# Top-32 attention into routed experts: row scans folded to half width, mask and product moved to GpSimd, row sums to ScalarE

## The chip, the core and the metric

The kernel runs on one core of one Trainium2 chip. The metric is device time in microseconds: the median of five runs, and beside it one execution taken with the profiler, whose trace the readings come from. Engines are named as the profile names them: PE (TensorE), PEld (its weight loads), DVE (VectorE), ACT (ScalarE), POOL (GpSimd), SP (SyncE, which issues most DMAs).

## The reference

Inputs are float32: `q`, `k`, `v` of 8 batches x 8 heads x 576 rows x 64, a gate of 512 x 8, and for 8 experts `w1` (512 x 1024) and `w2` (1024 x 512).

```python
scores = scale * np.matmul(q, k.transpose(0, 1, 3, 2))
kth = np.partition(scores, -32, axis=-1)[..., -32:-31]
scores = np.where(scores >= kth, scores, -1e9)
attn = np.exp(scores - scores.max(-1, keepdims=True))
attn = attn / (attn.sum(-1, keepdims=True) + 1e-09)
x = matmul(attn, v), heads side by side          # 4608 x 512
expert = argmax(x @ w_gate); gate = its softmax probability
out = gate * (relu(x @ w1[expert]) @ w2[expert])
```

So in each of 36,864 score rows of 576 the 32nd largest value is a threshold; what lies below it gets no weight.

## The kernel before

**Attention.** Two heads share the 128 partitions; a unit is one pair of heads of one batch, 32 units in all. A unit's 1152 query rows make nine tiles of 128 rows: four groups of two (the same chunk of both heads), and one single tile that holds the last 64 rows of both. For each group `scores` multiplies q and k into PSUM (L182) and ScalarE copies the 128 x 576 result to SBUF as `s` (L188). `weights` finds the threshold on DVE: four rounds of MAX8 (L200, the eight largest of a row) with three match-replaces between them (L205, which overwrite those eight). After the first round GpSimd makes the bias from the row maximum (L202), and ScalarE computes the exponential `ex` (L203). DVE then compares, multiplies and sums in one instruction, `w = (s >= threshold) * ex` with its row sum in `z` (L212).

`transposed` turns `w` on PE (four transposes at L223, the tail at L224) and ScalarE copies the results to `wT` and `wTt` (L228 to L232). After the ninth tile `outputs` multiplies with v in two halves (`po`, L253), copies to `oT` (L254), transposes back to `px` (L261) and DVE scales by the reciprocal row sums into `x` (L262, the tail at L269).

**Routing.** After every second batch `route` transposes `x` (L283), computes gate logits (L287), copies them (L291), finds each token's expert and its place, and writes token numbers to lists in HBM by nine indirect DMAs from GpSimd's queue (L326). `x` goes to HBM from SP's queue (L339, L342).

**Experts.** 25 slots of 256 tokens each: SP reads a list piece and the expert's weights, GpSimd gathers rows (L434), PE multiplies twice (L452, L459), GpSimd scatters the result (L464). Two slots are loaded ahead.

**Order.** The code asks for the scores of the next group ahead of the weights of this one, and for transposes of the last tile after the weights of this one. A scheduler then sets the order on each engine, and each engine works its queue in order. Pools bound what may run ahead: four buffers of `s`, three of `w`, two of `ex`, two score tiles in PSUM.

Of the kernel before, what the change touches and what calls it, by code (L numbers as in the profile page):

```python
# [1 line left out]

# [12 lines left out]
TOP_K = 32  # L15
NEG = -3.0e38
EPS = 1e-9


def _ins(ap: bass.AP, axis: int, n: int) -> bass.AP:  # L20
    dims = [list(d) for d in ap.ap]
    dims.insert(axis, [0, n])
    return bass.AP(tensor=ap.tensor, offset=ap.offset, ap=dims)

# [6 lines left out]
def kernel(  # L31
# [9 lines left out]
):  # L41

# [70 lines left out]
    tok_id = []  # L113
    for p in range(NP):
        t = const.tile([P, NT], I32, name=f"tok_id{p}")
        b0 = 2 * p * S
        nc.gpsimd.iota(t[:, 0:NC], pattern=[[P, NC]], base=b0, channel_multiplier=1)
        nc.gpsimd.iota(t[:, NC:2 * NC], pattern=[[P, NC]], base=b0 + S, channel_multiplier=1)
        nc.gpsimd.iota(t[0:ST, 2 * NC:NT], pattern=[[1, 1]], base=b0 + SM, channel_multiplier=1)
        nc.gpsimd.iota(t[ST:P, 2 * NC:NT], pattern=[[1, 1]], base=b0 + S + SM, channel_multiplier=1)  # L120
        tok_id.append(t)

# [10 lines left out]
    cnt = None  # L133
    firstp = ctx.enter_context(tc.tile_pool(name="firstp", bufs=1))
    first_w = None

    with (
        tc.tile_pool(name="pad", bufs=1) as padp,
        tc.tile_pool(name="load", bufs=2) as load,
        tc.tile_pool(name="att", bufs=2) as att,  # L140
        tc.tile_pool(name="wtp", bufs=2) as wtp,
        tc.tile_pool(name="xp", bufs=2) as xp,
        tc.tile_pool(name="small", bufs=3) as small,
        tc.tile_pool(name="ps_s", bufs=2, space=bass.MemoryType.PSUM) as ps_s,
        tc.tile_pool(name="ps_w", bufs=2, space=bass.MemoryType.PSUM) as ps_w,
        tc.tile_pool(name="ps_1", bufs=1, space=bass.MemoryType.PSUM) as ps_1,
    ):
        qk, vs_of, xt, units = {}, {}, {}, {}

        def load_qk(b, u):  # L150
            qb = load.tile([P, 2, S], F32, name="qb")
            nc.sync.dma_start(qb, qt[b, u * P:(u + 2) * P, :].rearrange("(u p) s -> p u s", p=P))
            kb = load.tile([P, 2, S], F32, name="kb")
            nc.sync.dma_start(kb, kt[b, u * P:(u + 2) * P, :].rearrange("(u p) s -> p u s", p=P))
            for n in range(2):
                qk[b, u + n] = (qb[:, n, :], kb[:, n, :])

        def load_v(b):
            vb = load.tile([P, KC, HD], F32, name="vb")
            nc.sync.dma_start(vb[:, 0:NC, :], vt[b, 0:SM, :].rearrange("(c p) d -> p c d", p=P))  # L160
            nc.sync.dma_start(vb[0:ST, NC, :], vt[b, SM:S, :])
            vs_of[b] = vb

        def parts(i):

            if i < 2 * NC:
                h, c = divmod(i, NC)
                return [(h, slice(0, P), slice(c * P, (c + 1) * P))]
            return [(h, slice(h * ST, (h + 1) * ST), slice(SM, S)) for h in range(2)]

        def scores(b, u, tiles):
            qu, ku = qk[b, u]
            todo = []
            got = []
            for i in tiles:
                ps = ps_s.tile([P, 2, SM], F32, name="sc")
                todo += [(ps, h, rows, cols) for h, rows, cols in parts(i)]
                got.append(ps)
            for j in range(2):
                for ps, h, rows, cols in todo:  # L180
                    d = slice(h * D, (h + 1) * D)
                    nc.tensor.matmul(  # L182
                        ps[rows, j, 0:HF], qu[d, cols], ku[d, j * HF:(j + 1) * HF], start=True, stop=True
                    )
            out_s = []
            for ps in got:
                s = att.tile([P, 2, HF], F32, name="s", bufs=4)
                nc.scalar.copy(s, ps[:, :, 0:HF])  # L188
                out_s.append(s)
            return out_s  # L190

        def weights(b, u, i, s3):
            s = s3[:, :, :].rearrange("p j k -> p (j k)")
            tops = small.tile([P, TOP_K // 8, 8], F32, name="tops")
            scr = att.tile([P, S], F32, name="scr")
            nbias = small.tile([P, 1], F32, name="nbias")
            ex = att.tile([P, S], F32, name="ex")
            src = s
            for r in range(TOP_K // 8):
                nc.vector.max(out=tops[:, r, :], in_=src)  # L200
                if r == 0:
                    nc.gpsimd.tensor_scalar(nbias, tops[:, 0, 0:1], -scale, None, ALU.mult)  # L202
                    nc.scalar.activation(ex, s, AF.Exp, scale=scale, bias=nbias)  # L203
                if r < TOP_K // 8 - 1:
                    nc.vector.match_replace(  # L205
                        out=scr, in_to_replace=tops[:, r, :], in_values=src, imm_value=NEG
                    )
                    src = scr
            w = att.tile([P, S], F32, name="w", bufs=3)
            z = units[b, u][2]  # L210
            c = 2 * NC if i == 2 * NC else 2 * (i % NC) + i // NC
            nc.vector.scalar_tensor_tensor(  # L212
                out=w, in0=s, scalar=tops[:, TOP_K // 8 - 1, 7:8], in1=ex,
                op0=ALU.is_ge, op1=ALU.mult, accum_out=z[:, c:c + 1],
            )
            return w

        def transposed(b, u, i, w):
            wT, wTt, _ = units[b, u]
            pm = ps_w.tile([P, NC, P], F32, name="wTm")  # L220
            pt = ps_1.tile([P, SM], F32, name="wTl")
            for c in range(NC):
                nc.tensor.transpose(pm[:, c, :], w[:, c * P:(c + 1) * P], ident)  # L223
            nc.tensor.transpose(pt[0:ST, 0:P], w[:, SM:S], ident)  # L224
            if i < 2 * NC:
                h, c = divmod(i, NC)
                q = slice(c * P, (c + 1) * P)
                nc.scalar.copy(wT[:, :, h, q], pm)  # L228
                nc.scalar.copy(wTt[:, h, q], pt[0:ST, 0:P])
            else:  # L230
                nc.scalar.copy(wT[:, :, :, SM:S], pm[:, :, :].rearrange("p c (h q) -> p c h q", h=2))
                nc.scalar.copy(wTt[:, :, SM:S], pt[0:ST, 0:P].rearrange("p (h q) -> p h q", h=2))  # L232

        def outputs(b, u):
            vb = vs_of[b]
            wT, wTt, z = units[b, u]
            rz = small.tile([P, NT + 1], F32, name="rz", bufs=2)
            nc.vector.tensor_scalar_add(rz[:, 0:NT], z, EPS)
            nc.vector.reciprocal(rz[:, 0:NT], rz[:, 0:NT])
            nc.vector.tensor_copy(rz[0:ST, NT:NT + 1], rz[ST:P, 2 * NC:NT])  # L240
            oT = att.tile([P, S], F32, name="oT")
            for j in range(2):
                q = slice(j * HF, (j + 1) * HF)
                po = ps_1.tile([P, SM], F32, name="po")
                for c in range(KC):
                    for h in range(2):
                        rows = slice(h * D, (h + 1) * D)
                        vs = slice(u * P + h * D, u * P + (h + 1) * D)
                        if c < NC:
                            lhsT, rhs = vb[:, c, vs], wT[:, c, h, q]  # L250
                        else:
                            lhsT, rhs = vb[0:ST, c, vs], wTt[:, h, q]
                        nc.tensor.matmul(po[rows, 0:HF], lhsT, rhs, start=(c == 0), stop=(c == KC - 1))  # L253
                nc.scalar.copy(oT[:, q], po[:, 0:HF])  # L254
            p, half = divmod(b, 2)
            if u == 0 and half == 0:
                xt[p] = xp.tile([P, NT, XW], F32, name="x")
            x = xt[p]
            px = ps_1.tile([P, SM], F32, name="px", tag="po")
            for t in range(NC):  # L260
                nc.tensor.transpose(px[:, t * P:(t + 1) * P], oT[:, t * P:(t + 1) * P], ident)  # L261
            nc.vector.tensor_tensor(  # L262
                x[:, half * NC:(half + 1) * NC, u * P:(u + 1) * P].rearrange("p t (h d) -> p t h d", h=2),
                px[:, :].rearrange("p (t h d) -> p t h d", t=NC, h=2),
                _inner(rz[:, 0:2 * NC].rearrange("p (t h) -> p t h", h=2), D), op=ALU.mult,
            )
            pl = ps_1.tile([P, SM], F32, name="pl", tag="po")
# [247 lines left out]
```

## Time and profile before

| what | value |
|---|---|
| median of five runs | 2674.95 us (2673.63 to 2678.48) |
| profiled execution | 2674.07 us, its span 2672.4 us |
| mean granted TensorE clock | 0.715 |
| DVE busy | 1736.5 us (65%) |
| PE busy, PEld busy | 2039.0 us (76%), 1206.3 us (45%) |
| ACT busy | 717.4 us (27%) |
| POOL busy | 200.7 us (8%) |

A line of a group gives the source line, engine, operation, output and inputs with shapes, the count, then busy time in us and mean ns of one, then the idle time of the engine just before them and what ended it. A timeline line gives the start, the duration, and in brackets the idle time before it and the releaser. A stretch gives its borders and length, then PE, PEld, DVE, ACT and POOL busy with counts, the granted clock, the DMA share and GB/s.

### The profile page before, as it was taken

Reading aid. Unit: us, or ns where it says so; the run is one execution under the profiler, and the core shown is the slowest. Engines: PE = TensorE matmul, PEld = TensorE weight load, DVE = VectorE, ACT = ScalarE, POOL = GpSimd, SP = SyncE. Lnnn points to the kernel's source line nnn. Section 1 sums busy time; section 2 is a strip of 40 time slices with the busy share of each in tenths; the row PEclk is TensorE's granted clock in tenths of the full one; section 3 lists DMA queues with packets and bytes.
Section 4 is the critical chain, followed back from the end, with each engine's and each line's share of the span. In section 5 each row is a group of like instructions: output and inputs, shape, how many; then the busy total and the mean of one; then the engine's idle time right before and its main releaser. Section 6 shows DMA issues by size and latency. Waiting matters only on the chain. (4 is left out here: it accounts for less than half of the span.)

```text
span 2672.4 us, 22208 instructions
## 1 busy us (share of the span) xinstructions
PE 2039.0 (76%) x7208; PEld 1206.3 (45%) x7208; DVE 1736.5 (65%) x3864; ACT 717.4 (27%) x1457; POOL 200.7 (8%) x453
## 2 busy tenths in 40 slices
PE   5767767666767776677686667676199999999998
PEld 3334334333333543333353333334166666666665
DVE  8999998699999869999986999995100010010000
ACT  3333333233333323333332333332011011001100
POOL 0000000100000010000001000000111111111110
PEclk7665566566666656665665666665599999999999
DMA  3000001100000110000011000000364444545440
GB/s 136 18 18 18 18 1 36 36 18 18 18 18 0 36 36 18 18 18 18 0 36 36 18 18 0 1 0 0 116 226 161 179 174 179 181 159 198 158 155 2
DMA packets 71172, 166.84 MB, mean 62 GB/s; under 512 B 9612, under 2 KB 9740, under 8 KB 71058
## 3 DMA queue, kind: packets, MB, share of 16 engines
q1 hardware_dynamic: 61906, 142.83, 15.8%
q0 software_dynamic: 9152, 22.60, 2.2%
q8 instruction: 58, 0.95, 0.1%
q14 instruction: 56, 0.46, 0.1%
HBM read 146.34 MB, written 22.73 MB: 63 GB/s over the span
## 5 line engine op out<-in xcount | busy, mean ns | idle before, releaser
L223 PE MATMUL wTm<-ident,w 128*128 128x128 f32 x1152 | 282.3, 392 | 493.2 <-DVE w L212 476.5
L200 DVE MAX8 tops<-scr 128x8 f32<-128x576 f32 x864 | 620.1, 744 | 0.5
L182 PE MATMUL sc<-kb,qb 64*128 64x288 f32 (+1 forms) x1280 | 577.1, 656 | 30.2 <-ACT s L188 22.6
L223 PEld LDWEIGHTS wTm<-ident,w 128*128 128x128 f32 x1152 | 187.8, 199 | 670.9 <-issue 504.9
L205 DVE MATCH_REPLACE8 scr<-tops,scr 128x576 f32<-128x576 f32 x576 | 424.9, 738 | 0.0
L182 PEld LDWEIGHTS sc<-kb,qb 64*128 64x128 f32 (+1 forms) x1280 | 279.7, 269 | 202.2 <-issue 108.1
L452 PE MATMUL ph<-xTs,w 128*128 128x256 f32 x1600 | 353.9, 382 | 14.1 <-DVE xTs L447 13.5
L188 ACT COPY s<-sc 128x576 f32<-128x576 f32 x288 | 184.1, 640 | 646.7 <-DVE w L212 638.0
L459 PE MATMUL py<-w,hT 128*128 128x512 f32 x800 | 347.4, 592 | 0.0
L452 PEld LDWEIGHTS ph<-xTs,w 128*128 128x128 f32 x1600 | 303.5, 191 | 60.4 <-DVE xTs L447 19.0
L463 DVE TENSOR_SCALAR y<-py,xg 128x512 f32<-128x512 f32 x50 | 37.5, 750 | 440.8 <-PE py L459 440.8
L253 PE MATMUL po<-wT,vb 128*64 128x288 f32 x1024 | 275.5, 638 | 1.4 <-ACT wT L228 0.9
L455 ACT ACTIVATE hT<-ph 128x256 f32<-128x256 f32 x200 | 76.6, 383 | 701.7 <-PE ph L452 701.7
L203 ACT ACTIVATE ex<-s,nbias 128x576 f32<-128x576 f32 x288 | 223.8, 777 | 92.8 <-POOL nbias L202 92.7
L459 PEld LDWEIGHTS py<-w,hT 128*128 128x128 f32 x800 | 152.0, 190 | 180.7 <-issue 179.4
L212 DVE SCALAR_TENSOR_TENSOR w<-s,tops,ex 128x576 f32<-128x576 f32 x288 | 230.0, 800 | 0.1
L200 DVE MAX8 tops<-s 128x8 f32<-128x576 f32 x288 | 213.7, 743 | 8.5 <-ACT s L188 8.4
L205 DVE MATCH_REPLACE8 scr<-tops,s 128x576 f32<-128x576 f32 x288 | 212.5, 738 | 0.0
L228 ACT COPY wT<-wTm 128x512 f32<-128x512 f32 x256 | 149.9, 586 | 169.5 <-PE wTm L223 166.1
L202 POOL TENSOR_SCALAR nbias<-tops 128x1 f32<-128x1 f32 x288 | 60.5, 210 | 1665.9 <-DVE tops L200 1365.5
L253 PEld LDWEIGHTS po<-wT,vb 128*64 128x64 f32 x1024 | 108.5, 213 | 163.1 <-issue 156.9
L431 DVE TENSOR_SCALAR src<-idx 128x2 int32<-128x2 int32 x25 | 4.2, 169 | 262.4 <-DMA idx<-lists 262.4
(89 smaller groups left out, 983.4 us busy)
## 6 DMA issues: line engine op xcount, KB each, us to landing
w<-in_moe_w_dram SPq DMA_DIRECT2D x50, 2048.0 KB, 11.2
qb<-in_qt_dram SPq DMA_DIRECT2D x16, 576.0 KB, 3.9
kb<-in_kt_dram SPq DMA_DIRECT2D x16, 576.0 KB, 4.9
x_rows<-x SPq DMA_DIRECT2D x8, 1026.0 KB, 10.3
vb<-in_vt_dram SPq DMA_DIRECT2D x8, 1024.0 KB, 5.8
x_rows<-x SPq DMA_DIRECT2D x8, 128.2 KB, 10.4
vb<-in_vt_dram SPq DMA_DIRECT2D x8, 128.0 KB, 5.7
xg<-x_rows,src POOLq DMA_INDIRECT x50, 7.8
```

What stands on the lines that cost most here:

```text
L182: nc.tensor.matmul(ps[rows, j, 0:HF], qu[d, cols], ku[d, j * HF:(j + 1) * HF], start=True, stop=True)
L188: nc.scalar.copy(s, ps[:, :, 0:HF])
L200: nc.vector.max(out=tops[:, r, :], in_=src)
L203: nc.scalar.activation(ex, s, AF.Exp, scale=scale, bias=nbias)
L205: nc.vector.match_replace(out=scr, in_to_replace=tops[:, r, :], in_values=src, imm_value=NEG)
L212: nc.vector.scalar_tensor_tensor(out=w, in0=s, scalar=tops[:, TOP_K // 8 - 1, 7:8], in1=ex, op0=ALU.is_ge, op1=ALU.mult, accum_out=z[:, c: ...
L223: nc.tensor.transpose(pm[:, c, :], w[:, c * P:(c + 1) * P], ident)
L228: nc.scalar.copy(wT[:, :, h, q], pm)
L253: nc.tensor.matmul(po[rows, 0:HF], lhsT, rhs, start=(c == 0), stop=(c == KC - 1))
L452: nc.tensor.matmul(ph, w1[:, 0, dt, f * P:(f + 1) * P], xT[:, dt, :], start=(dt == 0), stop=(dt == DT - 1))
L455: nc.scalar.activation(hT[:, f, :], ph, AF.Relu)
L459: nc.tensor.matmul(py, hT[:, f, c * P:(c + 1) * P], w2[:, 0, f, :], start=(f == 0), stop=(f == FT - 1))
```

## The change

Each score row is folded: DVE writes the maximum and the minimum of `s[i]` and `s[i + 288]` to `hl`. The four rounds of MAX8 and three match-replaces run over the 288 larger members, and one more MAX8 over the smaller members. The 32nd largest of all is then the largest of nine minima: the (32 - j)th of the larger with the jth of the smaller, j from 0 to 8. This is exact while at most eight of the smaller members belong to the top 32.

The difference of the eighth smaller member and the threshold is kept in `over`, and its maximum in `doubt`. After attention this becomes a flag. After the experts each engine loads the flag and branches: where it is raised, a second copy of the kernel (full-width scans, in loops) computes everything again.

The comparison with the threshold and the product with `ex` are now two instructions on GpSimd, and the row sum is an activation on ScalarE. `weights` and the transposes work on a whole group, not on one tile; `ex` has four buffers instead of two, `scr` three instead of two, `x` one instead of two. The thresholds' scratch `tops` is four tiles used in turn. Gate, routing and expert code move into functions without other change.

```diff
+    def scores(b, u, tiles):
...
             s = k.att.tile([P, 2, HF], F32, name="s", bufs=4)
             nc.scalar.copy(s, ps[:, :, 0:HF])
+            if not k.exact:
+                hl = k.att.tile([P, 2, HF], F32, name="hl", bufs=4)
+                nc.vector.tensor_tensor(hl[:, 0, :], s[:, 0, :], s[:, 1, :], op=ALU.max)
+                nc.vector.tensor_tensor(hl[:, 1, :], s[:, 0, :], s[:, 1, :], op=ALU.min)
...
+    def weights(b, u, tiles, ss):
...
+            src = [hl[:, 0, :] for _, hl in ss]
...
+        for r in range(R):
+            for m in range(n):
+                nc.vector.max(out=tops[:, m, r * 8:(r + 1) * 8], in_=src[m])
+            if r == 0:
+                nc.gpsimd.tensor_scalar(nbias[:, 0:n], tops[:, 0:n, 0], -scale, None, ALU.mult)
+                for m in range(n):
+                    nc.scalar.activation(ex[m], s[m], AF.Exp, scale=scale, bias=nbias[:, m:m + 1])
+                if not k.exact:
+                    for m in range(n):
+                        nc.vector.max(out=tops[:, m, TOP_K + 1:TOP_K + 9], in_=ss[m][1][:, 1, :])
+            if r < R - 1:
+                for m in range(n):
+                    nc.vector.match_replace(
...
+            both = k.small.tile([P, 2, 9], F32, name="both")
+            nc.vector.tensor_tensor(
+                both[:, 0:n, :], _back(tops[:, 0:n, TOP_K - 9:TOP_K]), tops[:, 0:n, TOP_K:TOP_K + 9], op=ALU.min
+            )
+            nc.vector.tensor_reduce(thr[:, 0:n], both[:, 0:n, :], axis=AX.X, op=ALU.max)
+            nc.gpsimd.tensor_tensor(over[:, c:c + n], tops[:, 0:n, TOP_K + 8], thr[:, 0:n], op=ALU.subtract)
...
-            nc.vector.scalar_tensor_tensor(
-                out=w, in0=s, scalar=tops[:, TOP_K // 8 - 1, 7:8], in1=ex,
-                op0=ALU.is_ge, op1=ALU.mult, accum_out=z[:, c:c + 1],
-            )
+            w = k.att.tile([P, S], F32, name="w", bufs=3)
+            nc.gpsimd.tensor_scalar(w, s[m], thr[:, m:m + 1], None, ALU.is_ge)
+            nc.gpsimd.tensor_tensor(w, w, ex[m], op=ALU.mult)
+            nc.scalar.activation(ex[m], w, AF.Copy, accum_out=z[:, c + m:c + m + 1])
...
+        nc.vector.tensor_tensor(doubt, doubt, over, op=ALU.max)
...
+    again = nc.values_load(any_i[0:1, 0:1], min_val=0, max_val=P)
+    with tc.If(again > 0):
...
```

The order that the scheduler gives the changed kernel, in the steady part of a unit: DVE runs the first MAX8 of the next pair around the threshold of this one, then its fifth MAX8s and first match-replaces, then the folds of the pair after next. GpSimd runs for each pair: bias of the next pair, `over`, two comparisons, two products. ScalarE runs: one exponential, two score copies, two row sums, the second exponential, then the copies of transposes. PE runs the transposes of a pair, then scores of a later group; in two of the four pairs three score matmuls stand between the second tile's transposes and its tail transpose.

## The prediction

> **What bounds the kernel now.** I read the totals and slices first, then the stretches of time, then groups of instructions by shape, then the timeline of one pair and of one unit's end.
>
> ```profile
> PE 2039.0 (76%) x7208; PEld 1206.3 (45%) x7208; DVE 1736.5 (65%) x3864; ACT 717.4 (27%) x1457; POOL 200.7 (8%) x453
> DVE  8999998699999869999986999995100010010000
> PEclk7665566566666656665665666665599999999999
> ```
>
> Two stages show. The DVE row is nearly full for 28 of 40 slices and empty after, the clock row low, then full. Stretches of time give the borders (columns: stretch, its length, busy us with instruction counts):
>
> ```profile
> 0.00:1838.00 1838.00, 1288.23 (x4466) 703.12 (x4466) 1654.88 (x3690) 634.16 (x1244) 92.78 (x344) 0.61 0.07 22
> 1936.00:2672.00 736.00, 716.86 (x2587) 476.62 (x2585) 69.51 (x121) 76.60 (x200) 95.36 (x96) 1.00 0.45 162
> ```
>
> Attention takes about 1838 us, DVE busy 1655 of them, PE 1288 at a granted clock of 0.61. Last route, list reading and experts (1838 to 2672) keep their instructions, and I let them stand. What DVE does per row tile:
>
> ```profile
> L200 DVE MAX8 tops<-scr 128x8 f32<-128x576 f32 x864 | 620.1, 744 | 0.5
> L205 DVE MATCH_REPLACE8 scr<-tops,scr 128x576 f32<-128x576 f32 x576 | 424.9, 738 | 0.0
> L212 DVE SCALAR_TENSOR_TENSOR w<-s,tops,ex 128x576 f32<-128x576 f32 x288 | 230.0, 800 | 0.1
> L401 DVE TENSOR_TENSOR past<-slots,end 1x175 f32<-1x175 f32 x1 | 0.3, 322 | 0.0
> ```
>
> Instructions overlap by about 0.07 us: in the timeline one MAX8 starts 0.67 after another, a match-replace with its value load takes 0.72, the product 0.73. A tile is 4 x 0.67 + 3 x 0.72 + 0.73 = 5.57 us, a pair 11.14; the timeline has 721.28 to 732.40 = 11.12 between like products. Nine tiles are 50.1. Starts of the scaling at L262 (698.97, 753.57) lie 54.6 apart; of the other 4.5, 3.1 to 3.2 is one wait, the rest small work:
>
> ```profile
> 697.82 0.40 ACT L254 COPY oT<-po 128x288 f32<-128x288 f32 x1 [5.42 <-PE po L253]
> 698.97 0.69 DVE L262 TENSOR_TENSOR x<-px,rz 128x512 f32<-128x512 f32 x1 [3.20 <-PE px L261]
> ```
>
> So a unit is 54.6 us, 32 make 1747; the three routes inside stretch the spacing to 84.5, 82.1 and 84.5.
>
> **DVE after.** Removed: L212 and half the width of every scan. Halving 576 elements saves 0.30 us of each (175 elements take 0.32 us and 72 take 0.22, L316, in the two-input rows, so 1.0 ns an element): MAX8 0.37, match-replace 0.42 with its load. Added: two folds of 288, 0.32 + 113 x 0.001 = 0.43 each, 0.36 start to start, and a fifth MAX8. A tile is 2 x 0.36 + 5 x 0.37 + 3 x 0.42 = 3.83; each group adds a minimum and a maximum over 18 elements, 0.25 together by the 9-element rows (0.16 to 0.19). A pair is 7.9, the single tile 4.1, small work 1.5 with the doubt maximum: 37.2 a unit without waits.
>
> **GpSimd after.** Before, it makes one bias per tile (L202, 0.21 us for one element). No row shows a wide comparison or product there. Nearest: the 128-element select at L95 takes 0.288, the 288-element iota at L348 0.373 against 0.134 for 4, so 0.6 to 0.85 ns an element. The comparison is 0.21 + 575 x that = 0.56 to 0.70; I take 0.7, as it reads and compares like the select but by a per-row value. The product reads two operands: twice the slope, 0.9 to 1.2; I take 1.2, and 2.0 as the upper end since no two-input row bounds it. By the Trainium skill (GPSIMD Engine Reference, Elementwise — side-by-side cycle accounting), a two-input add of 2048 takes 4497 ns there; scaled, an estimate of 1.27 us, which would add 0.14 to a pair; no row here shows it. With bias and flag (0.2 each, the bias mostly early) a pair is about 4.1 us from the threshold to its second product, 19 us per unit: no bound by volume. Its place counts: it is now between DVE's threshold and PE's transposes.
>
> **ScalarE after.** The row sum is a 576-wide activation like L203 (0.777), plus a read of the accumulator (0.08 on DVE): 0.85 per tile. Per tile 0.64 + 0.78 + 0.85 + 0.59 + 0.26 = 3.1, 28 per unit: below DVE. But it waits in order for the second product, and behind it in its queue stand an exponential, the copies of transposes, and the next score copies.
>
> **The shared port.** Folds read two SBUF inputs. What that does to GpSimd shows where a scatter starts under L212, also two inputs:
>
> ```profile
> 501.04 0.80 DVE L212 SCALAR_TENSOR_TENSOR w<-s,tops,ex 128x576 f32<-128x576 f32 x1
> 501.15 1.57 POOL L326 DMA_INDIRECT lists<-tok_id,posi  x1 [4.46 <-DMA lists<-tok_id,posi]
> 520.43 0.97 POOL L326 DMA_INDIRECT lists<-tok_id,posi  x1 [2.33 <-DMA lists<-tok_id,posi]
> ```
>
> The first takes 0.6 more, and 501.04 + 0.80 - 501.15 = 0.69 of L212 was left. Five more that start under it take 1.07 to 1.23; nearly all others take 0.97 to 1.03. GpSimd stands still for the rest of L212. Under MAX8 a bias at 537.65 takes its usual 0.21. The reverse, DVE waiting for GpSimd, doesn't show: L212 at 968.45, in the middle of a scatter, starts on time and takes 0.80; but a scatter isn't elementwise work. So a fold's wait for a running GpSimd instruction is bounded by 0 and one product, 1.2. In the changed order the folds of the pair after next stand 1.6 us behind a threshold (two MAX8, two match-replaces), and their score buffers come free by the two comparisons (1.0 and 1.7), just when the products begin. I take one wait and 0.4 for a late score copy, 1.6 per pair: 9.5.
>
> In half the pairs a loop is longer: second product, transposes 1.09, three score matmuls 3.4 (2.29 for two), the tail transpose 0.42, its copy 0.26, exponential 0.78, score copy 0.64, hand-overs 0.3: 6.9 us. It must fit into a period and 1.6. With the product at 4.1 it asks 9.4, at 5.6 (one wait) 10.9; by the fast rows (1.23, 0.66, 0.27) 2.2 less, 7.2 to 8.7. I take 9.9 for those pairs, 9.7 over all.
>
> **Unit's end.** Before, 9.3 us run from the last product (689.7) to L262, 6.1 covered by DVE's next work. After, GpSimd adds 2.2 and a score matmul 0.5 to 1.1: 12 to 12.6; DVE's cover is 7.35 (ten MAX8, five match-replaces, two folds, small ones) plus 1.5 of port waits: 3.5 left.
>
> **Sum.** A unit: 4 x 9.7 + 5.2 (single, with one short wait) + 1.5 + 3.5 = 49.0 against 54.6; 32 x 5.6 = 179 off. Routes: DVE has 9.4 instead of 12 us of cover before the logits, and their nine scatters now queue ahead of comparisons and products, each waiting for the one before to land (1.9 to 4.5); bounds 0 and 20, I take 8 each, 24. The end gains a register load and a branch per engine, no row for it: 0 to 8, I take 4, since the second path is skipped. In the inputs of the reference I counted, of 36,864 rows, how many smaller pair members reach the threshold: at most 6, and 8 raise the flag. The profiled execution is 2674.07 (span 2672.4 and 1.7 around it), 0.9 below the median of the five runs, so nothing is shifted: 2674 - 179 + 24 + 4 = 2523, given as 2525.
>
> **Rivals.** (1) Full gain: folds don't wait, and denser PE work earns a higher clock. Unit 37.2 + 3 = 40.2, 32 x 14.4 = 461 off, 12 on: about 2225, up to 2400 with half the waits. For it: the L212 that started on time; PE's idle stretches of 3 to 5 us in attention would shrink, and the expert stage, where PE is busy 717 of 736 us, is granted 1.00. Against: the folds come exactly when products run. (2) Slower: DVE and GpSimd alternate, fold, product, fold, so a pair waits twice, and the second product slips to 7. Pairs are then 11.1, those with the loop 12.3, the single 6, unit's end 5: unit 59.3, 32 x 4.7 = 150 on, with 28 gives 2852; about 2800 if some pairs escape. It decides from a pair mean of 10.7 on ((53.7 - 5.5 - 1.5 - 4) / 4, with 54.6 less 28/32). A product of 2.0 instead of 1.2 leads there too. For it: GpSimd's full stop under L212. Against: neighbouring DVE instructions overlap, so the second fold may keep the port. By the Trainium skill (SBUF — State Buffer, Who interferes with whom), a DVE instruction with two SBUF inputs and a GpSimd one that reads SBUF exclude each other, whichever starts first holding the port throughout; that speaks for this rival. The scatters agree in one direction (1.57 against 0.97); the other is unseen here. (3) The flag is raised and the second path runs: at least another 2600 us; the count speaks against it.
>
> **Chances.** Forecast 0.45 (2430 to 2640), full gain 0.17, slower 0.34, second path 0.01, break-even 0.03. About 0.2%, 5 us, is what a measurement here can tell. Faster 0.62, same 0.03, slower 0.35 (with the second path). The range 2320 to 2790 leaves out half of the full gain and about 0.1 of the slow side; the forecast alone spans 2430 to 2640.
>
> **What would show it.** Right: pairs 9.3 to 10.2 apart on DVE, folds with idle before them put to GpSimd or ScalarE, MAX8 near 444 ns, GpSimd about 0.7 and 1.2, L262's wait 3 to 4. Wrong: pairs near 8 (full gain); products of 2 us, or pairs over 10.7 with the long wait at score copies (slower); instructions of the second path in the trace.

## Result

The changed kernel takes 2682.28 us (median of 31 runs, 2664.19 to 2691.65) against 2676.37 us of the kernel before (55 runs); the ratio is 1.0023, with a 95% interval of 1.0016 to 1.003. The forecast was 2525 us; the kernel came out slower by 0.2% instead of faster by 6%, inside the range and on its other side.

The profiled execution took 2680.86 us, its span 2679.0. The totals and slices of the page after:

```profile
PE 2063.3 (77%) x7210; PEld 1179.0 (44%) x7210; DVE 1410.0 (53%) x4511; ACT 910.7 (34%) x2033; POOL 1109.8 (41%) x1062
...
DVE  7777777478777747777775777774100010010000
...
PEclk9656666556566656565665565666599999999999
```

VectorE's work did go: 1410 us busy instead of 1737. GpSimd's went from 201 to 1110. But the DVE row, which stood at 8 and 9 through attention, stands at 7 for as many slices as before. The two stretches of the prediction, in its columns:

```profile
0.00:1838.00 1838.00, 1311.40 (x4461) 675.48 (x4461) 1328.21 (x4335) 824.29 (x1811) 997.60 (x950) 0.62 0.07 22
1936.00:2672.00 736.00, 719.57 (x2597) 478.66 (x2596) 71.56 (x123) 76.60 (x200) 95.15 (x96) 1.00 0.45 164
```

In the same 1838 us VectorE is busy 1328 us instead of 1655, and what it stopped doing became idle time. The clock (0.62) and the expert stretch are as before. The last scaling of `x` (L329, which was L262) starts at 1849.2 against 1846.2, and what follows takes 829.8 us against 826.2; together these are the 6.6 us of the span. The groups of instructions by shape:

```profile
L277 POOL TENSOR_SCALAR w<-s,thr 128x576 f32<-128x576 f32 x288 | 493.6, 1723 | 65.0 <-PE wTl L289 65.0
...
L278 POOL TENSOR_TENSOR w<-w,ex 128x576 f32<-128x576 f32 x288 | 410.0, 1441 | 3.4
L245 DVE MAX8 tops<-scr 128x8 f32<-128x288 f32 x864 | 353.9, 444 | 0.1
...
L223 DVE TENSOR_TENSOR hl<-s 128x288 f32<-128x288 f32 x288 | 199.6, 693 | 351.9 <-ACT s L219 351.9
...
L224 DVE TENSOR_TENSOR hl<-s 128x288 f32<-128x288 f32 x288 | 181.9, 632 | 0.5
```

The scans are what was forecast. The comparison (L277) takes 1.72 us, more than the product (1.44), and the folds (L223, L224) average 0.69 and 0.63 instead of the 0.43 that was reckoned. The first fold has 352 us of idle time before it. Of the waits (engine, tile and line, what it waited for, us in total, times, longest) three lines matter:

```profile
DVE hl L223 <- ACT s L219: 351.9, 219, 10.3
...
ACT s L219 <- POOL w L277: 171.5, 157, 3.7
...
DVE x L329 <- PE px L328: 107.1, 31, 5.7
```

352 us are 11.0 us per unit, slightly more than the 327 us by which VectorE's busy time fell in attention. The second line gives the next link: ScalarE's score copies wait for the comparisons, the last readers of the score buffers. A pair in the timeline shows how it comes about (start, duration; in brackets the idle time before and its releaser):

```profile
713.29 0.14 DVE L271 TENSOR_REDUCE thr<-both 128x2 f32<-128x18 f32 x1
...
713.81 3.43 POOL L277 TENSOR_SCALAR w<-s,thr 128x576 f32<-128x576 f32 x2
...
715.57 0.64 ACT L219 COPY s<-sc 128x576 f32<-128x576 f32 x1 [1.08 <-POOL w L277]
716.24 0.46 DVE L223 TENSOR_TENSOR hl<-s 128x288 f32<-128x288 f32 x1 [1.23 <-ACT s L219]
...
717.20 2.98 POOL L278 TENSOR_TENSOR w<-w,ex 128x576 f32<-128x576 f32 x2
717.27 0.64 ACT L219 COPY s<-sc 128x576 f32<-128x576 f32 x1 [1.06 <-POOL w L277]
717.94 0.98 DVE L223 TENSOR_TENSOR hl<-s 128x288 f32<-128x288 f32 x1 [0.87 <-ACT s L219]
...
718.84 1.66 DVE L224 TENSOR_TENSOR hl<-s 128x288 f32<-128x288 f32 x1
...
725.10 0.15 DVE L271 TENSOR_REDUCE thr<-both 128x2 f32<-128x18 f32 x1
```

The threshold is computed at 713.29. VectorE goes on with the next pair's first scans until 715.01; then the folds of the pair after next stand in its order. Their score copies need the two buffers that the comparisons still read, until about 715.5 and 717.2. Each copy starts as a comparison ends, and each first fold starts as its copy ends: 1.23 and 0.87 us idle. By now the products run, and the last two folds take 0.98 and 1.66 us. From threshold to threshold it is 11.81 us. The working closes: 7.9 without waits, 2.10 idle, 1.76 in which those two folds hold up what follows (0.90 and 1.58 from start to start instead of 0.36 each), 11.76 together.

### The profile page after: what moved, and what is told of

It is laid out like the page before. It is cut to its first block, busy times and chain, and to the rows that moved or that the text cites. A ratio compares the mean times of both kernels' runs of the same rounds, so it can differ in the third digit from the quotient of the medians.

```text
span 2679.0 us, 24033 instructions
## 1 busy us (share of the span) xinstructions
PE 2063.3 (77%) x7210; PEld 1179.0 (44%) x7210; DVE 1410.0 (53%) x4511; ACT 910.7 (34%) x2033; POOL 1109.8 (41%) x1062
## 5 line engine op out<-in xcount | busy, mean ns | idle before, releaser
L213 PE MATMUL sc<-kb,qb 64*128 64x288 f32 (+1 forms) x1280 | 568.6, 649 | 255.4 <-ACT s L219 248.0
L277 POOL TENSOR_SCALAR w<-s,thr 128x576 f32<-128x576 f32 x288 | 493.6, 1723 | 65.0 <-PE wTl L289 65.0
L213 PEld LDWEIGHTS sc<-kb,qb 64*128 64x128 f32 (+1 forms) x1280 | 253.1, 259 | 462.6 <-ACT s L219 297.0
L278 POOL TENSOR_TENSOR w<-w,ex 128x576 f32<-128x576 f32 x288 | 410.0, 1441 | 3.4
L223 DVE TENSOR_TENSOR hl<-s 128x288 f32<-128x288 f32 x288 | 199.6, 693 | 351.9 <-ACT s L219 351.9
L245 DVE MAX8 tops<-scr 128x8 f32<-128x288 f32 x864 | 353.9, 444 | 0.1
L499 POOL DMA_INDIRECT out_dram<-y,idx x50 | 50.5, 1011 | 620.0 <-DVE y L498 620.0
L279 ACT ACTIVATE ex<-w 128x576 f32<-128x576 f32 x288 | 197.3, 686 | 208.8 <-POOL w L278 208.8
L255 DVE MATCH_REPLACE8 scr<-tops,scr 128x288 f32<-128x288 f32 x576 | 250.0, 438 | 0.0
L247 POOL TENSOR_SCALAR nbias<-tops 128x2 f32<-128x2 f32 (+1 forms) x160 | 46.9, 293 | 408.0 <-DVE thr L271 366.2
L224 DVE TENSOR_TENSOR hl<-s 128x288 f32<-128x288 f32 x288 | 181.9, 632 | 0.5
## 6 DMA issues: line engine op xcount, KB each, us to landing
w<-in_moe_w_dram SPq DMA_DIRECT2D x50, 2048.0 KB, 10.7
```

Source lines behind the costliest of these rows:

```text
L213: nc.tensor.matmul(ps[rows, j, 0:HF], qu[d, cols], ku[d, j * HF:(j + 1) * HF], start=True, stop=True)
L223: nc.vector.tensor_tensor(hl[:, 0, :], s[:, 0, :], s[:, 1, :], op=ALU.max)
L245: nc.vector.max(out=tops[:, m, r * 8:(r + 1) * 8], in_=src[m])
L255: nc.vector.match_replace(out=scr[m], in_to_replace=tops[:, m, r * 8:(r + 1) * 8], in_values=src[m], imm_value=NEG,)
L277: nc.gpsimd.tensor_scalar(w, s[m], thr[:, m:m + 1], None, ALU.is_ge)
L278: nc.gpsimd.tensor_tensor(w, w, ex[m], op=ALU.mult)
```

## Experiments

Theory A: GpSimd's comparison is slow by itself, holds the score buffers and delays the products. Theory B: GpSimd's work on SBUF stretches VectorE's folds through the shared port. Theory C: folded scans bring nothing here. Theory D was formed after the first runs: four score buffers leave the copies no lead, so that whatever is late on their way stops VectorE.

**Folds alone.** Mask, product and row sum are one VectorE instruction again.

```diff
-            nc.gpsimd.tensor_scalar(w, s[m], thr[:, m:m + 1], None, ALU.is_ge)
-            nc.gpsimd.tensor_tensor(w, w, ex[m], op=ALU.mult)
-            nc.scalar.activation(ex[m], w, AF.Copy, accum_out=z[:, c + m:c + m + 1])
+            nc.vector.scalar_tensor_tensor(
+                out=w, in0=s[m], scalar=thr[:, m:m + 1], in1=ex[m],
+                op0=ALU.is_ge, op1=ALU.mult, accum_out=z[:, c + m:c + m + 1],
+            )
```

> The changed kernel with the comparison, product and row sum back in one DVE instruction; folded scans, flag and second path stay. Theory A (GpSimd's long comparison holds the loop up) and theory B (folds and GpSimd exclude each other at the shared port) both expect DVE to set the pace: a tile 3.83 + 0.73 = 4.56 us, a unit 9 x 4.56 + 1.3 + 1.5 + 3 = 47, so 32 x 7.6 = 243 off the kernel before, 2440. If the folded scans themselves brought nothing (theory C: waits inside the scans), it would stay over 2600.

Measured: 2418.01 us, ratio 0.9011 (0.8989 to 0.9032). C falls: the folded scans are worth a tenth of the time, and moving the mask away gives it back. Both folds average 0.45 us, and VectorE's wait for score copies is 88 us in all.

**GpSimd's operations alone.** The kernel before, with comparisons, products and the like over 64, 288 and 576 elements ahead of attention, one after another.

```diff
+        for name, n in (("m64", 64), ("m288", HF), ("m576", S)):
+            tb = padp.tile([P, S], F32, name=name)
+            nc.gpsimd.tensor_scalar(tb[:, 0:n], ta[:, 0:n], ones[:, 0:1], None, ALU.is_ge)
...
+            nc.gpsimd.tensor_tensor(tb[:, 0:n], ta[:, 0:n], ta[:, 0:n], op=ALU.mult)
```

> The kernel before, with GpSimd instructions added ahead of attention, where DVE is idle: comparison and product by a per-row value and by a constant, a maximum, a subtract-and-multiply and two-input product and subtraction, each over 64, 288 and 576 elements. Theory A (the comparison is slow by itself): the comparison by a per-row value over 576 takes about 1.7 us here too, the two-input product 1.4. Theory B (the shared port stretches it): the comparison takes about 0.7 and the product 1.2, as forecast.

The groups there (L348 is the comparison by a per-row value, L353 the product):

```profile
L348 POOL TENSOR_SCALAR m<-ta,ones 128x576 f32<-128x576 f32 x1 | 1.7, 1733 | 0.0
...
L353 POOL TENSOR_TENSOR m<-ta 128x576 f32<-128x576 f32 x1 | 1.1, 1140 | 0.0
...
L348 POOL TENSOR_SCALAR m<-ta,ones 128x64 f32<-128x64 f32 x1 | 0.5, 467 | 0.1
```

This kernel takes 2693.47 us in all (one run). The comparison takes 1.73 us alone as well. VectorE is idle beside it, so its price is its own, not the port's: (1733 - 467) / 512 = 2.5 ns an element. The product, 1.14 us, is nearer to B's 1.2 than to A's 1.4.

**A short comparison.** It covers 64 of 576 columns, and the product squares the exponential: this kernel leaves out the mask.

```diff
-            nc.gpsimd.tensor_scalar(w, s[m], thr[:, m:m + 1], None, ALU.is_ge)
-            nc.gpsimd.tensor_tensor(w, w, ex[m], op=ALU.mult)
+            nc.gpsimd.tensor_scalar(w[:, 0:64], s[m][:, 0:64], thr[:, m:m + 1], None, ALU.is_ge)
+            nc.gpsimd.tensor_tensor(w, ex[m], ex[m], op=ALU.mult)
```

> The changed kernel, its comparison over only 64 of 576 columns, its product of the exponential with itself over all 576: the mask is left out, the instruction count and the order of waits stay. Theory A: score buffers come free at 0.8 us after a threshold instead of 3.8 and the second product at 3.7 instead of 6.6; the forecast's sum then holds, 2480 to 2560. Theory B: products still exclude folds, more than 2620.

Measured: 2636.92 us, ratio 0.9838 (0.9813 to 0.9862): A missed. The total misleads, though. Unit spacings, without the route units and the three behind them, fell from 54.3 to 48.3 on average, and attention ended 87.0 us earlier although those six took 479 us instead of 416. Then the time after attention was 870.5 us instead of 829.8. Without the mask the routing differs; that the longer lists and experts come from that is likely, and was not separated. The comparison's length is worth some 6 us of the 54 of a unit, less than the 11 that VectorE waits. VectorE still waits 293.5 us for score copies here, and its folds, 0.71 and 0.73 us, are stretched more than before.

**Folds from PSUM.** One half of each fold is read where the score matmul left it.

```diff
-                nc.vector.tensor_tensor(hl[:, 0, :], s[:, 0, :], s[:, 1, :], op=ALU.max)
-                nc.vector.tensor_tensor(hl[:, 1, :], s[:, 0, :], s[:, 1, :], op=ALU.min)
+                nc.vector.tensor_tensor(hl[:, 0, :], ps[:, 0, 0:HF], s[:, 1, :], op=ALU.max)
+                nc.vector.tensor_tensor(hl[:, 1, :], ps[:, 0, 0:HF], s[:, 1, :], op=ALU.min)
```

> The changed kernel, the folds reading one half of a score row from PSUM and one from SBUF, so that they have one SBUF input; everything else stays. Theory A: only the folds' own waits go, 576 folds at 0.45 are 259 of their 381 us, so at most 4 us a unit, 120 in all, and likely less as the score copies still come late: 2600 to 2680. Theory B: below 2560.

Measured: 2600.81 us, ratio 0.9698 (0.9682 to 0.9714). In its timeline a fold inside two products now takes its usual time:

```profile
730.61 2.79 POOL L278 TENSOR_TENSOR w<-w,ex 128x576 f32<-128x576 f32 x2
...
732.33 0.45 DVE L223 TENSOR_TENSOR hl<-sc,s 128x288 f32<-128x288 f32 x1
```

So the stretches need both of a fold's inputs in SBUF, as B has it. They were 199.6 + 181.9 - 576 x 0.445 = 125 us; without them the kernel gains 82. But its folds still wait 413 us for score copies, and the time is not below the 2560 that B asked for: B is real, and the smaller part.

**The comparison on VectorE.** It takes 0.51 us there.

```diff
-            nc.gpsimd.tensor_scalar(w, s[m], thr[:, m:m + 1], None, ALU.is_ge)
+            nc.vector.tensor_scalar(w, s[m], thr[:, m:m + 1], None, ALU.is_ge)
```

> The changed kernel with the comparison alone moved to VectorE (one instruction for 576 scores); the product stays on GpSimd, the row sum on ScalarE. VectorE gains 288 comparisons; a fold of half the width takes 0.45, so I estimate 0.4 to 0.8 us each, 115 to 230 us in all, or 3.6 to 7.2 us per unit. Theory A (the price of the comparison on GpSimd, 1.72 us also when it runs alone, is what cost the gain): the wait for score copies nearly goes, units of 46 to 50 us, 2420 to 2540 us. Theory B (any GpSimd work on the score rows stretches VectorE's two-input work, and the product alone is enough): folds keep means over 600 ns and the time is over 2580 us.

Measured: 2656.32 us, ratio 0.989 (0.9873 to 0.9908). A in its strong form falls: the slow comparison is gone, and plain units still take 54.0 us. The wait for score copies is 258 us, in 65 long ones:

```profile
L224 DVE TENSOR_TENSOR hl<-s 128x288 f32<-128x288 f32 x288 | 201.1, 698 | 0.4
...
L223 DVE TENSOR_TENSOR hl<-s 128x288 f32<-128x288 f32 x288 | 154.6, 537 | 258.5 <-ACT s L219 258.5
```

B's numbers came out: the folds average 0.62 us over both lines, and the time is over 2580. But the stretches, 201.1 + 154.6 - 256 = 100 us, are less than half of that wait. One of the long waits in the timeline:

```profile
726.81 0.40 ACT L321 COPY oT<-po 128x288 f32<-128x288 f32 x1 [7.38 <-PE po L320]
...
727.78 0.63 ACT L219 COPY s<-sc 128x576 f32<-128x576 f32 x1
...
728.45 0.46 DVE L223 TENSOR_TENSOR hl<-s 128x288 f32<-128x288 f32 x1 [7.11 <-ACT s L219]
```

Here the score copy stands behind the copy of an output row on ScalarE, which waits for the output matmuls. The waiting line is the same, but what stands ahead of the copy is another.

**Eight score buffers.**

```diff
-            s = k.att.tile([P, 2, HF], F32, name="s", bufs=4)
+            s = k.att.tile([P, 2, HF], F32, name="s", bufs=8)
```

> The changed kernel with eight buffers for `s` instead of four; nothing else. In the changed kernel VectorE waits 351.9 us in all for score copies, and in a plain unit the copies of a later pair begin when a comparison (1.72 us each) has let go of a score buffer, while the folds of that pair stand ahead of scans that could run. Theory A (the long comparison holds the score buffers): the 171.5 us in which ScalarE's score copies wait for comparisons go to under 30 us and the wait of the folds falls by at least 130 us, so 2500 to 2580 us. Rival (the loop of product, transposes, score matmuls and copies binds at the same place; the buffer is only the last of several that end there): the copies then wait for another releaser and the time stays at 2640 to 2700 us.

Measured: 2379.56 us, ratio 0.8862 (0.8847 to 0.8877): better than both theories allowed, and better than both kernels. Its groups:

```profile
L219 ACT COPY s<-sc 128x576 f32<-128x576 f32 x288 | 182.7, 637 | 232.4 <-POOL w L277 218.5 <-PE sc L213 12.9 <-DVE hl L224 0.8
...
L224 DVE TENSOR_TENSOR hl<-s 128x288 f32<-128x288 f32 x288 | 161.9, 562 | 0.0
...
L223 DVE TENSOR_TENSOR hl<-s 128x288 f32<-128x288 f32 x288 | 148.4, 515 | 9.5 <-ACT s L219 9.2
```

VectorE's wait for score copies is 9 us instead of 352. The comparison is still 1.74 us, and score copies wait for it longer than before (218 us against 171): in the first line the wait stays, but it costs nothing, since the copies now run ahead of the folds. The expectation looked for the gain in ScalarE's wait, which did not fall; VectorE's did. A unit is 44.4 us: 37.2 of work, 1.7 of stretched folds (148.4 + 161.9 - 256, over 32), and 2.7, 1.8 and 1.1 for the waits at L329, L305 and L336 (84.9, 56.6 and 35.3 us in all). The steps from threshold to threshold in a unit, from the second pair on (the fourth step starts at the single tile, and the last holds the unit's end), are 7.8, 7.3, 7.8, 8.3 and 13.4 where the changed kernel has 11.8, 10.0, 9.8, 7.5 and 13.9.

**The mask's move alone.** The first pass at full width, with the mask on GpSimd.

```diff
-        open_pools(st, 2, False)
+        open_pools(st, 2, True)
```

> The changed kernel with its first pass at full width: no folds, no second list, MAX8 and match-replace over 576, while the comparison and the product stay on GpSimd and the row sum on ScalarE (the second, flagged pass is the same code as before). It shows the move of the mask by itself. VectorE loses 0.90 us per tile against the kernel before (the mask instruction and its accumulator read), 8.1 us per unit, and has no two-input instruction left in a pair. If the mask's path through GpSimd binds a unit wherever the scans end (theory A in its strong form), units stay at 53 to 55 us and the time is 2640 to 2720 us. If only folds caught between comparisons and products lose time (theory B), pairs are 9.5 to 10 us, units 47 to 50 us and the time 2430 to 2540 us.

Measured: 2677.23 us, ratio 0.9976 (0.9966 to 0.9986). Without a fold in the kernel, VectorE loses 9 x 0.73 = 6.6 us of work per unit, and units go from 54.4 to 53.8. The first MAX8 waits 148 us for score copies, which wait 427 us for comparisons. That is what A in its strong form expected, and B alone can't explain it; full width with eight buffers was not run.

**Folds from PSUM, mask on VectorE.** The edits of the version with folds alone and of the one with folds from PSUM, together.

> Folds that read one half of the row in PSUM and the other in SBUF, with mask, product and row sum in one VectorE instruction again, and nothing else on GpSimd than the small steps. Against the version with folds only (2418 us), in which the folds took 451 to 453 ns, nothing disturbs a fold: both theories expect the same time within 20 us, 2400 to 2440 us. If the first operand in PSUM lengthens a fold (over 500 ns), up to 2460 us.

Measured: 2449.35 us, ratio 0.9115 (0.9099 to 0.9131), 31 us over the version with folds only, although the folds take 0.45 us as there: more than either theory allowed. VectorE's wait for score copies is 117 us instead of 88, and score matmuls now wait for folds (14 us are put to L224).

**Eight buffers, comparison on VectorE.** Both edits shown above.

> The version with the comparison on VectorE, now with eight buffers for `s` as well. With four it took 2656 us although its comparison takes 0.47 us, and in the unit that I read its long wait for a score copy (7.1 us) stands behind the copy of an output row on ScalarE, which waits for the output matmuls. Theory D (with four buffers a score copy cannot run ahead of whatever happens to be late on its way, and the folds stand in VectorE's order ahead of scans that could run; which releaser is named last does not matter): the 258 us of waits for score copies fall under 40 us, and the time is the version with eight buffers plus 288 comparisons on VectorE less some waits, 2400 to 2500 us. Rival E (in this version something else than the lead binds, the product on GpSimd or the output matmuls): over 2600 us.

Measured: 2389.3 us, ratio 0.8901 (0.8885 to 0.8916). D holds: 267 us go, and the wait for score copies is again 9 us. The lower end that was expected, 2400, was undershot: the added comparisons (140 us busy) came in as other waits went (those at L329, L305 and L336 are 42 us in all, and 177 with eight buffers alone), and a unit is 44.2 us. The folds are stretched about as much as with four buffers (0.57 and 0.62 us, 87 us in all), so it was not B that cost those 267 us.

**Eight buffers in the kernel before.**

```diff
-                s = att.tile([P, 2, HF], F32, name="s", bufs=4)
+                s = att.tile([P, 2, HF], F32, name="s", bufs=8)
```

> The kernel before with eight buffers for `s` instead of four; nothing else. It tells whether the gain of eight buffers belongs to this change. In the kernel before the scans fill the pairs (9 x 5.57 = 50.1 of 54.6 us) and no wait of VectorE for a score copy is among its long ones. Theory D: at most the idle time of a unit, 3.5 to 4.5 us, can be had: 2560 to 2690 us. Rival: four buffers held any version back, the kernel before as well: under 2500 us.

Measured: 2692.91 us, ratio 1.0025 (1.0016 to 1.0035), nothing gained, and slightly over what D allowed. Score copies wait 638 us for the mask in the kernel before, and VectorE, which runs the mask in its own order, waits 8 us for score copies. The need for buffers belongs to the change.

**Eight buffers, folds alone.** The edits of those two versions together.

> The version with folds only (mask, product and row sum in one VectorE instruction, 2418 us) with eight buffers for `s`. Its folds waited 88 us for score copies with four. Theory D: these go and little comes back, 2330 to 2390 us. Rival: the waits there stand at the end of a unit and are ended by the outputs whatever the buffers, 2400 to 2430 us.

Measured: 2370.9 us, ratio 0.8825 (0.8808 to 0.8841), the fastest of all. A plain unit is mostly 43.3 to 43.5 us, and VectorE is busy for 43.2 of 43.3 (37.2 + 9 x 0.73 = 43.8 by the forecast's prices): nothing is left to wait for.

**Eight buffers, folds from PSUM.** Again both edits together.

> Eight buffers for `s` (2380 us) and folds that read one half from PSUM. With eight buffers alone the two folds still average 515 and 562 ns where 445 to 453 are undisturbed ones: 288 x (0.07 + 0.115) = 53 us of stretches left beside GpSimd's products. Theory B in what is left of it: these 53 us go, 2310 to 2350 us. Rival: folds that read PSUM hold the scores' PSUM buffers until VectorE comes to them (in the version with the mask on VectorE that cost 31 us, 2449 against 2418), so the copies lose the lead that eight buffers gave, and the time is 2390 us or more.

Measured: 2612.97 us, ratio 0.9727 (0.9711 to 0.9744). The rival was right, and by far more than its number. Its waits:

```profile
DVE hl L223 <- ACT s L219: 389.7, 97, 11.1
...
ACT s L219 <- PE sc L213: 226.7, 79, 7.6
PE sc L213 <- DVE thr L271: 183.2, 88, 4.1
```

The folds take 0.44 to 0.45 us, undisturbed, but they now hold the PSUM tile from which they read. The score matmuls wait for VectorE, the copies for the matmuls and the folds for the copies: the lead is gone whatever `s` has, and the time with it.

What is shown: the lost time is VectorE's wait for score copies. Eight buffers for `s` take it away, in two versions with different releasers of that wait, and tying the copies to PSUM brings it back. Two things stay open. The scheduler gives a kernel with eight buffers another order on the engines (VectorE's instructions agree with the changed kernel's, by line and operation, at 62% of the places). And the granted clock differs, as attention with eight buffers shows beside the 0.62 above:

```profile
0.00:1530.00 1530.00, 1103.94 (x4440) 600.67 (x4442) 1249.52 (x4335) 802.46 (x1809) 1028.59 (x949) 0.70 0.09 27
```

PE is busy 1104 us there instead of 1311 for nearly the same instructions; with the comparison on VectorE the clock goes from 0.59 to 0.69. A higher clock alone doesn't take the wait away: with folds from PSUM it is 0.69, and VectorE waits 413 us in units of 51.3. But how much of the 303 us is the buffers', the new order's or the clock's was not separated.

## Why the prediction was wrong

**Right.** VectorE's work per unit, 37.2 us: the account of the version with eight buffers closes on it. MAX8 at 444 ns and match-replace at 438 were the forecast 0.37 and 0.42 from start to start, the undisturbed fold 0.45. The wait at L329 is 107.1 us in 31, 3.45 each, where 3.5 was forecast. That is in part luck: in the unit whose L329 starts at 757.12, GpSimd takes 3.5 us from the threshold to the product where 2.2 was put, and the rest of the way to L329, 8.7 us, is 1.1 to 1.7 shorter than reckoned. The end cost 3.3 us (from the last scatter's start to the end of the span, 7.6 instead of 4.4) where 4 was taken. The flag did not lead to the second path.

**The step that failed** is the pair's "one wait and 0.4 for a late score copy". The late copies were sized at 0.4 a pair, less than 2 us a unit; they cost 351.9 / 32 = 11.0. The port was put at up to 1.2 a pair, and the stretches are 125 / 32 = 3.9 a unit, no more than forecast. In all, 14.9 us of these waits stand against the 8.3 in the sum (4 x 1.8 and 1.1 at the single tile). The difference of 6.6, on the forecast unit of 49.0, gives 55.6, where 54.4 was measured.

**Where the 0.4 came from.** It rests on the comparison: 0.7 us, read from a select of 128 elements and an iota. With 0.7 the score buffers come free 1.0 and 1.7 us after the threshold, about when the folds' turn comes at 1.6. The turn came at 1.7, but the comparisons, 1.72 each, ended 2.2 and 4.0 us after the threshold, and the copies only started then. No row of the trace showed a wide GpSimd operation. The product was given an upper end of 2.0 for that, the comparison only 0.56 to 0.70, as it reads one operand: the select at L95 is of another kind, and its slope did not carry over. The product came out at 1.44 beside the forecast 1.2 (the 1.27 that was estimated by the Trainium skill, GPSIMD Engine Reference, Elementwise — side-by-side cycle accounting, lies between its 1.14 alone and the 1.44), and from the threshold to the second product's end the pair above takes 6.9 us instead of 4.1.

The size alone was not the whole fault. With the comparison at 0.51 on VectorE the units stayed at 54.0, although this also gave VectorE some 4.3 us more work a unit (136 us over 32). The prediction priced the score copies by one chain of one pair, and let the second chain, the output copy on ScalarE, count only at the unit's end. It had named that the folds of the pair after next wait for these buffers; what it lacked was the question how late a copy may be before VectorE stops, which is the number of buffers.

**Routes.** 24 us were added; the spacings there are 84.5, 82.1 and 82.6 against 84.5, 82.1 and 84.5 before, so there was nothing to add. No queue past the scatters became late enough to show.

**The rivals.** The slower one had the sign and, in the prediction's last part, its mark in part: of the steps between the second, third and fourth pair one, 11.8, lies over 10.7 with the long wait at the score copies, and the other, 10.0, under it. Its mechanism was the lesser half: folds do wait for products, but its second ingredient was a slow product where it was a slow comparison, and 2852 was too far. The full gain (2225) was wrong for this kernel; its unit of 40.2 is 4 us below what eight buffers reach, though a higher clock, as it reckoned with, did come there (0.70). By the Trainium skill (SBUF — State Buffer, Who interferes with whom), a VectorE instruction with two SBUF inputs and a GpSimd instruction that reads SBUF exclude each other, and the first one holds the port throughout. The direction that was unseen before is seen now: of the 156 folds that start inside a product of the changed kernel half take 1.09 us or more. With the comparison the trace does not agree: 178 folds start inside one, at least 0.5 us ahead of its end; their median is 0.46 us and the longest takes 0.78. With eight buffers there are 118 such folds: half take about 0.45 and half 0.8 to 0.91, where waiting for the comparison's end would give at least 0.95. So some folds beside a comparison take longer, but none waited for its end. (The counts go by the start and duration of each single instruction in the traces.)

## What to carry to other kernels

When work moves to a slower engine, ask not only how long it takes there but which buffers it holds meanwhile, and whether the engine that you relieved has instructions in its order that need them; a wait in front of in-order work costs all that stands behind it. Test the lead first: more buffers on the producer's tile is a one-line edit, and here it showed that the comparison's 1.72 us could stay while the wait that it caused went. Try each half of a combined change alone; here the folds were worth 10% and the move of the mask nothing, even with the waits removed (ratios of 0.886 with it and 0.8825 without).

## What the runs showed that was not expected

- On GpSimd a one-input comparison by a per-row value is slower than a two-input product: 1.73 against 1.14 us over 576 elements alone; by a constant it took 1.66. In the kernel the product takes 1.4 where the folds read PSUM (2.79 for two, above). The lone one read a single tile twice, and so does the product of the version with the short comparison, which takes 1.21 us; so that may be most of the difference, but it was not tried by itself.
- VectorE does the same comparison in 0.51 us. Its whole mask, product and row sum takes 0.81 and 0.08 for the accumulator, less than GpSimd's comparison alone.
- A wait may grow while the time falls: the score copies' wait for comparisons went from 171 to 218 us as the kernel became 303 us faster.
